# Attention and two FFNs on one core: keys scaled when they are copied, maxima that come out negated, and other numbers for the planner

## The chip, the cores and the metric

The kernel runs on one core of a Trainium2 chip. The time is device microseconds of one execution; lower is better. The times shown are the median of three runs, and one further execution was taken with the hardware profiler.

## What is computed

A block-sparse attention over 2 batches of 8 heads, 768 positions and 64 dimensions: each query sees the keys less than 16 positions away and one summary key for each block of 32 (the maximum over the block, with log 32 added to its score). Its output goes through two FFNs.

```python
scores_l = scale * np.matmul(q, k.transpose(0, 1, 3, 2))
scores_s = scale * np.einsum('bhsd,bhnd->bhsn', q, k_sum) + np.log(block)
scores_l_m = np.where(mask_l, scores_l, -1000000000.0)
scores_all = np.concatenate([scores_l_m, scores_s], axis=-1)
scores_all = scores_all - np.max(scores_all, axis=-1, keepdims=True)
a = np.exp(scores_all)
a = a / (np.sum(a, axis=-1, keepdims=True) + 1e-09)
out = np.matmul(a, np.concatenate([v, v_sum], axis=2))
...
h = x @ w_in1;  x = (h * np.cos(h)) @ w_out1
h = x @ w_in2;  x = (h * np.clip(h + 3.0, 0.0, 6.0) / 6.0) @ w_out2
```

The scale is 1/8. The FFNs run over 1536 rows, 512 wide, with 2048 hidden columns; every operand is split in a high and a low part (hi, lo), and a product is three matmuls.

## The kernel before

**Tiles.** The attention works on 12 tiles of 128 queries (`front(u)` and `back(u)`, u from 0 to 11), with all 8 heads in one tile. `front` loads the queries (`qt`), copies the windows of keys of the tile beside the block maxima into `kcat` (two buffers), and lets TensorE (PE) write mask plus scores into two PSUM banks: an identity product puts the mask there (L561), then 16 small matmuls add the scores (L574). DVE takes the maximum over each head's 120 columns (L595) and turns it into `nmx`, minus scale times the maximum (L596); ACT computes the exponentials with `nmx` as bias, one instruction for each head (L604); DVE computes the reciprocal sums (L610, L611), and POOL or DVE multiplies (L614). `back` transposes the result through PE (L629), copies it into `pts`, and multiplies with the values `vcat` (L644); the outcome is split in `xhi` and `xlo`. The maxima over blocks are taken once for each batch (`prep_k`, L477) and copied beside the keys (`put_k`, L483); the means of the values come from products with a small averaging matrix (`prep_v`, L519).

**FFN.** The steps `s` of the plan are (FFN, block of 512 rows, slice of 128 hidden columns). The first 12 steps are narrow: 256 rows each, on the first eight tiles of the attention, run while the attention goes on. Step s is `mm1` (L780, the hidden column slice), `middle` (on ACT a rounding L843, on DVE L845, on ACT the sine L847, on DVE a product L849, then the split into `ghe` and `gle`) and `mm2` (L898). From the 13th step on PE works 512 columns wide, and the second FFN uses seven products instead of eight for a pair of slices (L731). Weights are converted on the way (`raw` to `cv_y` and `cv_t` to the `phi`, `plo`, `whi_out`, `wlo_out` parts).

**ACT's tables.** The exponential and the sine are in different table sets, so ACT runs an `ACT_TABLE_LOAD` whenever it goes from one to the other.

**What sets the order.** Nearly all of the work is recorded as operations of a `Graph` (`G.op`): the engines that may run it with a cost for each, what it reads and writes, and sometimes a due time. `Graph.forward` plays the operations through a timetable of its own and picks, for each engine, which operation comes next; `run` then writes the instructions in the order of their planned starts. These numbers belong to it:

```python
    PATIENCE = {"ACT": 0.3, "POOL": 0.0}
    UNWANTED, SWITCH = 1.0, 8.0
...
                        if other <= t + cost:
                            continue
                        urge += self.UNWANTED
                    if e == "ACT" and self.ops[i][4] not in (None, table):
                        cost += self.TABLE
                        urge += self.SWITCH
```

An operation that DVE and another engine can both do goes to DVE only where the other would end later by more than its PATIENCE, and then it stands back by UNWANTED microseconds; an operation for ACT that needs the other table stands back by SWITCH. Loads are operations of the queue SP, which issues in the planned order. Where the timetable shows PE a gap of more than 0.3 us and a matmul, `fill` puts matmuls over a tile of zeros there (L868, L873); 12 more warm PE up (L468).

Of the kernel before, what the change touches and what calls it, by code (L numbers as in the profile page):

```python
# [22 lines left out]
P = 128  # L23
# [13 lines left out]
class Graph:  # L37
# [10 lines left out]
    SAME = 0.16  # L48
    DMA_LATENCY = 1.8
    FIRST_DMA = 1.7  # L50
    TABLE = 1.3


    PATIENCE = {"ACT": 0.3, "POOL": 0.0}
    UNWANTED, SWITCH = 1.0, 8.0

    def __init__(self):
        self.filler = None
# [30 lines left out]
    def forward(self, due, succ):  # L89
        n = len(self.ops)  # L90
        missing = [len(o[2]) for o in self.ops]
        begins, ends, on = [0.0] * n, [0.0] * n, [None] * n
        free, table, port = {"SP": self.FIRST_DMA}, "exp", 0.0
        ready = {i: self.at[i] for i in range(n) if not missing[i]}
        order = []

        def start(i, e, at):
            t = max(free.get(e, 0.0), at)
            return max(t, port) if e == "POOL" or (e == "DVE" and self.twice[i]) else t

        while ready:
            starts, first = [], {}
            for i, at in ready.items():
                engines = self.ops[i][0]
                other = 1e9
                if "DVE" in engines and len(engines) > 1:
                    other = min(start(i, e, at) + c - self.PATIENCE[e] for e, c in engines.items() if e != "DVE")
                for e, cost in engines.items():
                    t = start(i, e, at)
                    urge = due[i]  # L110
                    if e == "DVE" and other < 1e9:
# [6 lines that stand above are left out]
                    starts.append((urge, t, i, cost, e))  # L118
                    if t < first.get(e, 1e9):
                        first[e] = t  # L120
            e = min(first, key=lambda e: (first[e], e))
            limit = first[e] + (0.1 if e != "PE" else 0.05)
            _, t, i, cost, _ = min(x for x in starts if x[4] == e and x[1] <= limit)
            del ready[i]
            begins[i], ends[i], on[i] = t, t + cost, e
            free[e] = ends[i]
            if e == "POOL" or (e == "DVE" and self.twice[i]):
                port = max(port, ends[i])
            if e == "ACT" and self.ops[i][4]:
                table = self.ops[i][4]  # L130
            order.append(i)
            for j in succ[i]:
                missing[j] -= 1
                if not missing[j]:
                    ready[j] = max(ends[d] + self.delay(d, j, on) for d in self.ops[j][2])
        return begins, ends, on, sorted(order, key=lambda i: begins[i])
# [52 lines left out]
def attention_two_ffn(  # L189
# [124 lines left out]
    qt = ring(kv, "qt", NQ, [P, HP, P])  # L314
    es = ring(kv, "es", NE, [P, 2, HP, KC])
    pts = ring(kv, "pts", 2, [KC, H, P])
    small = {n: ring(kv, n, 2, [P, H]) for n in ("mx", "nmx", "sm", "sme", "rs")}


    zero = const.tile([P, P], F32R, name="zero")  # L320
    nc.vector.memset(zero.bitcast(F32), 0.0)
    mask = es[NE - 1].rearrange("p j h c -> p (j h) c")[:, 0:3, :]

    more = math.log(BLK) / scale
    few = math.floor(more * 64.0) / 64.0
    nc.gpsimd.memset(mask, few - more)
    nc.gpsimd.memset(mask[:, :, WK:KC], few)
# [137 lines left out]
    def wake(n):  # L465

        for _ in range(n):
            nc.tensor.matmul(bank["d0"], zero, zero.unsqueeze(1).to_broadcast([P, NK, P]), start=True, stop=True)  # L468

    def load_kt(b):  # L470
        for hp in range(HP):
            G.op({"SP": dma(P * S * 4)}, lambda e, hp=hp: nc.sync.dma_start(
                out=ktile[0][:, hp, :], in_=kt[b, :, hp, :]), w=[("kt", hp)])
# [6 lines left out]

    def put_k(b, i):
        n = HP * 2 * NB
        G.op({"DVE": dve(n, 2), "POOL": one(n)}, lambda e: VEC[e].tensor_copy(  # L483
            kcat[i][:, :, :, WK:KC], ksum[b].unsqueeze(2).to_broadcast([P, HP, 2, NB])
        ), r=[("ks", b, hp) for hp in range(HP)], w=[("kcs", i)], twice=True)

    def vstage(t):
# [58 lines left out]
    def front(u):  # L546
# [31 lines left out]
        for z0, z1 in groups:  # L578
# [2 lines left out]
                ap=[list(ktile[0].ap[0]), [S, z1 - z0], [a[1] - a[0], 2], [1, WK]],  # L581
            )
            n = (z1 - z0) * 2 * WK
            G.op({"ACT": act(n), "DVE": dve(n, 2), "POOL": one(n)}, lambda e, z0=z0, z1=z1, keys=keys: copy(
                e, kc[:, z0:z1, :, 0:WK], keys),
                r=[("kt", hp) for hp in range(z0, z1)], w=[("kcw", k, hp) for hp in range(z0, z1)], twice=True)
            G.op({"PE": 1.02 * (z1 - z0) / HP}, lambda e, z0=z0, z1=z1: scores(z0, z1),
                 r=[("qt", qi), ("kcs", k)] + [("kcw", k, hp) for hp in range(z0, z1)], w=spk)
        ef = es[ei].rearrange("p j h c -> p (j h) c")
        mx, nmx, sm, sme, rs = (small[n][si] for n in ("mx", "nmx", "sm", "sme", "rs"))  # L590
        ek = [("e", ei, 0), ("e", ei, 1)]

        def largest(e):
            for j in range(2):
                nc.vector.tensor_reduce(mx[:, j * HP:(j + 1) * HP], s4[j], AX.X, ALU.max)  # L595
            nc.vector.tensor_scalar(nmx, mx, -scale, None, ALU.mult)  # L596

        G.op({"DVE": dve(H * KC) + 0.27}, largest, r=spk, w=[("mx", si)])

        def power(e):  # L600
            for j in range(2):
                for hp in range(HP):
                    c = j * HP + hp
                    nc.scalar.activation(ef[:, c, :], s4[j][:, hp, :], AF.Exp, bias=nmx[:, c:c + 1], scale=scale,  # L604
                                         accum_out=sm[:, c:c + 1])

        G.op({"ACT": 2.75}, power, r=[("mx", si)] + spk, w=ek + [("sm", si)], table="exp")
# [516 lines left out]
```

## Time and profile before

| | |
|---|---|
| median of 3 runs | 601.85 us (601.09 to 602.21) |
| the profiled execution | 602.27 us |
| its span, first to last instruction | 600.5 us |
| PE busy in the span | 589.0 us (98%) |
| DVE, ACT, POOL busy | 466.7, 353.8, 169.4 us |
| granted TensorE clock | 1.00 throughout |

An engine's busy time is the part of the span in which one of its instructions runs; loads, waits and register instructions are not counted. A busy PE is not PE at its peak, since matmuls overlap; and the matmuls over zeros are busy time too. The span is 1.77 us shorter than the execution's own time.

### The profile page before, as it was taken

Reading aid. Unit: us, or ns where it says so; the run is one execution under the profiler, and the core shown is the slowest. Engines: PE = TensorE matmul, PEld = TensorE weight load, DVE = VectorE, ACT = ScalarE, POOL = GpSimd, SP = SyncE. Lnnn points to the kernel's source line nnn. Section 1 sums busy time; section 2 is a strip of 40 time slices with the busy share of each in tenths; the row PEclk is TensorE's granted clock in tenths of the full one; section 3 lists DMA queues with packets and bytes.
Section 4 is the critical chain, followed back from the end, with each engine's and each line's share of the span. In section 5 each row is a group of like instructions: output and inputs, shape, how many; then the busy total and the mean of one; then the engine's idle time right before and its main releaser. Section 6 shows DMA issues by size and latency. Waiting matters only on the chain.

```text
span 600.5 us, 10003 instructions
## 1 busy us (share of the span) xinstructions
PE 589.0 (98%) x3845; PEld 502.2 (84%) x3845; DVE 466.7 (78%) x823; ACT 353.8 (59%) x738; POOL 169.4 (28%) x170
## 2 busy tenths in 40 slices
PE   9989999999999999999999999999999999999997
PEld 6568799888888888888888898898988989899896
DVE  4899888998787687667576999989869984984544
ACT  3898999786555455445456567667655543552321
POOL 4166645241000110010054475251123311410110
PEclk9999999999999999999999999999999999999999
DMA  8586534334122123012100220233301310200111
GB/s 294 180 269 216 168 108 141 106 108 138 57 85 71 35 71 105 1 35 71 35 1 0 71 63 9 91 122 106 105 32 41 141 70 1 71 0 1 71 72 70
DMA packets 17008, 51.50 MB, mean 86 GB/s; under 512 B 1984, under 2 KB 1984, under 8 KB 16960
## 3 DMA queue, kind: packets, MB, share of 16 engines
q1 hardware_dynamic: 16960, 50.86, 25.3%
q8 instruction: 30, 0.49, 0.4%
q14 instruction: 18, 0.15, 0.1%
HBM read 47.71 MB, written 3.15 MB: 85 GB/s over the span
## 4 chain that ended last, share of the span: by engine, by line
PE 80%; DVE 9%; ACT 9%; issue 1%; POOL 0%; DVEq 0%; ACTq 0%; POOLq 0%
PE bank_a L898 20%; PE bank_d L780 10%; PE bank_b L898 9%; PE bank_c L898 9%; PE bank_d L731 9%; PE bank_c L780 5%; PE bank_e L780 5%; PE bank_e L731 5%; PE bank_c L731 4%; ACT es L604 3%; DVE ch_c L854 2%; DVE mx L595 1%; PE bank_e L519 1%; PE bank_d L468 1%; DVE total L936 1%; ACT L847 1%
## 5 line engine op out<-in xcount | busy, mean ns | idle before, releaser
L460 POOL TENSOR_TENSOR cv_y<-cv_t,cv_y 128x512 int32<-128x512 int32 x25 | 34.6, 1386 | 129.9 <-ACT cv_y L441 64.6
L400 POOL TENSOR_TENSOR plo<-cv_y,phi 128x512 fp32r<-128x512 f32 (+1 forms) x19 | 24.4, 1283 | 128.6 <-DVE phi L383 118.9
L852 ACT ACTIVATE ch_c<-hs,three 128x512 f32<-128x512 f32 x48 | 33.9, 720 | 28.2 <-DVE hs L744 27.3
L383 ACT CAST ghi<-ch_c 128x512 fp32r<-128x512 f32 x61 | 37.4, 619 | 18.7 <-DVE ch_c L849 10.5
L458 DVE SCALAR_TENSOR_TENSOR cv_t<-raw,cv_t 128x512 int32<-128x512 int32 x64 | 47.1, 746 | 0.5
L744 DVE TENSOR_TENSOR hs<-bank_d,hs 128x256 f32<-128x256 f32 x60 | 25.3, 421 | 22.9 <-PE bank_d L731 22.1
L441 ACT ACTIVATE cv_y<-raw 128x512 int32<-128x512 uint32 x55 | 36.9, 674 | 10.5 <-DVE wlo_out L400 4.1
L451 ACT ACTIVATE cv_t<-raw 128x512 f32<-128x512 f32 x56 | 37.6, 672 | 8.7 <-DVE plo L400 3.7
L858 DVE TENSOR_TENSOR glo<-ch_c,ghi 128x512 fp32r<-128x512 f32 x53 | 36.5, 695 | 7.1 <-ACT ghi L383 6.2
L854 DVE SCALAR_TENSOR_TENSOR ch_c<-ch_c,hs 128x512 f32<-128x512 f32 x48 | 39.2, 827 | 3.4 <-ACT ch_c L852 1.9
L780 PE MATMUL bank_d<-xhi,phi 128*128 128x512 f32 (+1 forms) x136 | 35.3, 358 | 1.2 <-DVE xhi L383 0.7
L456 DVE TENSOR_SCALAR cv_t<-cv_t 128x512 int32<-128x512 int32 x64 | 33.1, 521 | 3.4 <-ACT cv_t L451 3.2
L858 POOL TENSOR_TENSOR glo<-ch_c,ghi 128x512 fp32r<-128x512 f32 x12 | 16.3, 1367 | 59.6 <-ACT ghi L383 52.8
L780 PE MATMUL bank_d<-xlo,phi 128*128 128x512 f32 (+1 forms) x136 | 32.1, 354 | 0.0
L780 PE MATMUL bank_d<-xhi,plo 128*128 128x512 f32 (+1 forms) x136 | 31.7, 354 | 0.2 <-DVE plo L400 0.2
L460 DVE CUSTOM_DVE_ANT_0 cv_y<-cv_t,cv_y 128x1024 uint16<-128x1024 uint16 x39 | 28.0, 725 | 1.8 <-ACT cv_y L441 0.9
L604 ACT ACTIVATE es<-bank_c,nmx 128x120 f32<-128x120 f32 x80 | 27.6, 371 | 1.9 <-DVE nmx L596 1.5
L780 PEld LDWEIGHTS bank_d<-xhi,phi 128*128 128x128 f32 x136 | 22.9, 188 | 5.8 <-DVE xhi L383 0.9
L780 PEld LDWEIGHTS bank_d<-xhi,plo 128*128 128x128 f32 x136 | 23.1, 188 | 4.8 <-issue 0.8
L847 ACT ACTIVATE ch_c<-ch_c,half_pi 128x512 f32<-128x512 f32 x25 | 18.0, 722 | 14.7 <-DVE ch_c L845 14.7
L780 PEld LDWEIGHTS bank_d<-xlo,phi 128*128 128x128 f32 x136 | 23.2, 189 | 3.7 <-DVE xlo L660 0.2
L383 ACT COPY hs<-bank_d 128x256 f32<-128x256 f32 x24 | 8.9, 372 | 25.1 <-PE bank_d L731 24.9
(343 smaller groups left out, 1846.1 us busy)
## 6 DMA issues: line engine op xcount, KB each, us to landing
raw<-in_w_in_dram SPq DMA_DIRECT2D x32, 512.0 KB, 3.4
raw<-in_w_out_dram SPq DMA_DIRECT2D x32, 512.0 KB, 3.3
vcat<-in_vw_dram SPq DMA_DIRECT2D x12, 384.0 KB, 4.2
ktile<-in_kt_dram SPq DMA_DIRECT2D x8, 384.0 KB, 5.4
qt<-in_q_dram SPq DMA_DIRECT2D x12, 256.0 KB, 4.7
out_dram<-total SPq DMA_DIRECT2D x8, 256.0 KB, 2.0
total<-in_vw_dram SPq DMA_DIRECT2D x6, 256.0 KB, 4.5
out_dram<-totak SPq DMA_DIRECT2D x4, 256.0 KB, 2.0
```

Of the source, the lines that this page charges most:

```text
L383: nc.scalar.copy(o, i) if e == "ACT" else VEC[e].tensor_copy(o, i)
L441: nc.scalar.activation(y, low.bitcast(U32), AF.Copy, scale=2.0 ** -29)
L451: nc.scalar.activation(o, a, AF.Copy, scale=2.0 ** -112)
L458: G.op({"DVE": dve(DM)}, lambda e: nc.vector.scalar_tensor_tensor(t, high, -0x80000000, t, ALU.bitwise_and, ALU.bitwise_or), r=[rk], w=[tk ...
L460: G.op({"POOL": pool(DM), "DVE": dve(DM)}, lambda e: VEC[e].tensor_tensor(y, t, y, ALU.add), r=[tk], w=[yk], twice=True)
L604: nc.scalar.activation(ef[:, c, :], s4[j][:, hp, :], AF.Exp, bias=nmx[:, c:c + 1], scale=scale, accum_out=sm[:, c:c + 1])
L731: nc.tensor.matmul(o, wt[i][:, A[a], kk * P:(kk + 1) * P], xt[:, kk, :], start=first and n + kk == 0, stop=n + kk == 3, skip_group_check=True)
L780: nc.tensor.matmul(h, w["in"][i][:, kk * P:(kk + 1) * P], x[blk][:, kk, c0:c1], start=p + kk == 0, stop=p == 2 and kk == NK - 1)
L852: G.op({"ACT": act(N)}, lambda e: nc.scalar.activation(c(), h(), AF.Relu, bias=three), r=hk, w=ck)
L854: G.op({"DVE": dve(N)}, lambda e: nc.vector.scalar_tensor_tensor(c(), c(), 6.0, h(), ALU.min, ALU.mult), r=hk, w=ck, twice=bool(both))
L858: G.op({"DVE": dve(N), "POOL": pool(N)}, lambda e: VEC[e].tensor_tensor(gbuf("lo", s)[:, 0:N], c(), gh().bitcast(F32), ALU.subtract), r=[* ...
L898: nc.tensor.matmul(acc(s, i)[0], l, r, start=first, stop=end and p == 2 and (N == TOK or i % 2 == 1), skip_group_check=N < TOK)
```

## The change

The scale goes into the key copies: `scaled` multiplies by 1/8 where the keys and the block maxima are copied into `kcat` (an activation on ACT, a tensor_scalar on DVE or POOL). The scores then come out of PE scaled, the mask's constants are scaled with them, the exponential needs no scale, and the reduction writes the maxima negated at once into `nmx`; the instruction of L596 and the tile `mx` are gone. The planner's numbers change: an issue takes 0.45 us of SP's time and may run ahead of the wire by 3 us, PATIENCE is exchanged between ACT and POOL, UNWANTED goes from 1 to 10 and SWITCH from 8 to 2. Its cost for the maxima is 0.2 us lower.

```diff
@@ -48,11 +48,12 @@
+    ISSUE, RUN_AHEAD = 0.45, 3.0
     TABLE = 1.3
-    PATIENCE = {"ACT": 0.3, "POOL": 0.0}
-    UNWANTED, SWITCH = 1.0, 8.0
+    PATIENCE = {"ACT": 0.0, "POOL": 0.3}
+    UNWANTED, SWITCH = 10.0, 2.0
...
@@ -124,6 +125,10 @@
             free[e] = ends[i]
+            if e == "SP":
+
+                ends[i] = wire = max(wire, t) + cost
+                free[e] = max(t + self.ISSUE, wire - self.RUN_AHEAD)
             if e == "POOL" or (e == "DVE" and self.twice[i]):
...
-    more = math.log(BLK) / scale
+    more = math.log(BLK)
...
+    def scaled(e, o, i):
+
+        if e == "ACT":
+            nc.scalar.activation(o, i, AF.Copy, scale=scale)
+        else:
+            VEC[e].tensor_scalar(o, i, scale, None, ALU.mult)
...
-        G.op({"DVE": dve(n, 2), "POOL": one(n)}, lambda e: VEC[e].tensor_copy(
-            kcat[i][:, :, :, WK:KC], ksum[b].unsqueeze(2).to_broadcast([P, HP, 2, NB])
+        G.op({"DVE": dve(n, 2), "POOL": one(n)}, lambda e: scaled(
+            e, kcat[i][:, :, :, WK:KC], ksum[b].unsqueeze(2).to_broadcast([P, HP, 2, NB])
...
-            G.op({"ACT": act(n), "DVE": dve(n, 2), "POOL": one(n)}, lambda e, z0=z0, z1=z1, keys=keys: copy(
+            G.op({"ACT": act(n), "DVE": dve(n, 2), "POOL": one(n)}, lambda e, z0=z0, z1=z1, keys=keys: scaled(
...
-                nc.vector.tensor_reduce(mx[:, j * HP:(j + 1) * HP], s4[j], AX.X, ALU.max)
-            nc.vector.tensor_scalar(nmx, mx, -scale, None, ALU.mult)
-
-        G.op({"DVE": dve(H * KC) + 0.27}, largest, r=spk, w=[("mx", si)])
+                nc.vector.tensor_reduce(nmx[:, j * HP:(j + 1) * HP], s4[j], AX.X, ALU.max, negate=True)
+
+        G.op({"DVE": dve(H * KC) + 0.07}, largest, r=spk, w=[("mx", si)])
...
-                    nc.scalar.activation(ef[:, c, :], s4[j][:, hp, :], AF.Exp, bias=nmx[:, c:c + 1], scale=scale,
+                    nc.scalar.activation(ef[:, c, :], s4[j][:, hp, :], AF.Exp, bias=nmx[:, c:c + 1],
```

The planner's numbers move rows on every engine. Three places follow. The first is on PE, at the end of the first tile's scores; the products with `avg` are the means of the values. Before:

```order
L574 MATMUL bank_c_96<-kcat_124,qt_129 64x120
L574 MATMUL bank_c_97<-kcat_124,qt_129 64x120
L574 MATMUL bank_c_96<-kcat_124,qt_129 64x120
L574 MATMUL bank_c_97<-kcat_124,qt_129 64x120
L519 MATMUL bank_e<-vnat_122,avg 32x512
L519 MATMUL bank_e<-vnat_123,avg 32x512
L574 MATMUL bank_a_93<-kcat_125,qt_130 64x120
```

and of the change:

```order
L586 MATMUL bank_c_97<-kcat_124,qt_129 64x120
L531 MATMUL bank_e<-vnat_122,avg 32x512
L586 MATMUL bank_c_96<-kcat_124,qt_129 64x120
L586 MATMUL bank_c_97<-kcat_124,qt_129 64x120
L586 MATMUL bank_c_96<-kcat_124,qt_129 64x120
L586 MATMUL bank_c_97<-kcat_124,qt_129 64x120
L531 MATMUL bank_e<-vnat_123,avg 32x512
L586 MATMUL bank_a_93<-kcat_125,qt_130 64x120
```

One of the two mean products now stands ahead of the last four of the 16 score matmuls.

The second is on ACT, from the table load ahead of the ninth tile of the exponentials (counted from 0) to the end of the tenth; `ch_e` is a narrow step's hidden tile (rounding with `quarter`, sine with `half_pi`). Before:

```order
L604 ACT_TABLE_LOAD
L604 ACTIVATE es_132,sm_142<-bank_c_96,nmx_140 128x120 x4
L604 ACTIVATE es_132,sm_142<-bank_c_97,nmx_140 128x120 x4
L383 COPY pts_135<-bank_b 120x512
L383 COPY total_91<-bank_a_94 128x2x256
L843 ACTIVATE ch_e_103<-bank_d_98,quarter 128x256
L441 ACTIVATE cv_y_82<-raw_68 128x512
L441 ACTIVATE cv_y_81<-raw_67 128x512
L383 COPY pts_135<-bank_b 120x512
L383 CAST whi_out_76<-cv_y_82 128x512
L604 ACTIVATE es_133,sm_141<-bank_c_96,nmx_139 128x120 x4
L604 ACTIVATE es_133,sm_141<-bank_c_97,nmx_139 128x120 x4
```

and of the change:

```order
L615 ACT_TABLE_LOAD
L615 ACTIVATE es_132,sm_140<-bank_c_96,nmx_138 128x120 x4
L615 ACTIVATE es_132,sm_140<-bank_c_97,nmx_138 128x120 x4
L854 ACTIVATE ch_e_103<-bank_d_98,quarter 128x256
L388 COPY pts_135<-bank_b 120x512
L456 ACTIVATE cv_t_84<-raw_68 128x512
L858 ACT_TABLE_LOAD
L858 ACTIVATE ch_e_103<-ch_e_103,half_pi 128x256
L446 ACTIVATE cv_y_82<-raw_68 128x512
L615 ACT_TABLE_LOAD
L615 ACTIVATE es_133,sm_139<-bank_c_96,nmx_137 128x120 x4
L615 ACTIVATE es_133,sm_139<-bank_c_97,nmx_137 128x120 x4
```

A sine with a table load on either side now stands between the two tiles, and copies of `pts`, `total` and `whi_out` have left ACT. From the fifth tile on it is so for each tile; ACT has 16 table loads in place of 12.

The third is on PE, behind the scores of the last tile (`qt_131`). Before:

```order
L574 MATMUL bank_c_97<-kcat_125,qt_131 64x120
L629 MATMUL bank_b<-ident,es_132 120x128 x4
...
L644 MATMUL bank_e<-pts_136,vcat_128 64x64 x16
L780 MATMUL bank_d_98<-xhi_86,phi_69 128x256 x4
L780 MATMUL bank_d_98<-xhi_86,plo_71 128x256 x4
L780 MATMUL bank_d_98<-xlo_89,phi_69 128x256 x4
L780 MATMUL bank_d_99<-xhi_86,phi_69 128x256 x4
```

and of the change:

```order
L791 MATMUL bank_d_98<-xhi_86,plo_71 128x256 x4
L791 MATMUL bank_d_98<-xlo_89,phi_69 128x256 x4
L640 MATMUL bank_b<-ident,es_132 120x128 x4
...
L573 MATMUL bank_c_97<-mask_hi,ident_r 128x480
L586 MATMUL bank_c_96<-kcat_125,qt_131 64x120
...
L586 MATMUL bank_c_97<-kcat_125,qt_131 64x120
L655 MATMUL bank_e<-pts_136,vcat_128 64x64 x16
```

The narrow step in `bank_d_98` (the eleventh of twelve) and a group of four transposes have moved ahead of the last mask and scores.

## Rows read from the trace of the kernel before

**Rows 1.** Busy time by stretch: length, PE, weight loads, DVE, ACT, POOL, clock.
```profile
0.00:25.00 25.00, 22.75 (x165) 14.60 (x169) 13.32 (x25) 14.20 (x48) 6.91 (x34) 1.00 0.68 222
25.00:50.00 25.00, 22.31 (x314) 17.86 (x312) 23.70 (x46) 22.14 (x83) 14.68 (x14) 1.00 0.77 254
50.00:75.00 25.00, 24.22 (x314) 18.90 (x313) 22.83 (x45) 23.29 (x63) 15.82 (x19) 1.00 0.63 201
75.00:100.00 25.00, 24.72 (x330) 22.35 (x329) 21.86 (x49) 23.82 (x77) 11.11 (x10) 1.00 0.37 119
100.00:125.00 25.00, 24.70 (x199) 21.78 (x198) 21.97 (x42) 21.47 (x46) 11.15 (x9) 1.00 0.35 115
125.00:150.00 25.00, 25.00 (x112) 20.71 (x111) 22.70 (x38) 16.56 (x27) 5.49 (x4) 1.00 0.37 126
```

**Rows 2.** The chain that ended last, its start: start us, us, what.
```profile
7.78 3.43 PE bank_d L868 x15
...
12.19 1.83 PE bank_e L519 x4
```

**Rows 3.** PE's weight loads in order of time behind tile 10's exponentials.
```profile
93.64 0.19 PEld L561 LDWEIGHTS bank_c<-mask_hi,ident_r 128*128 128x128 f32 x1 [0.22 <-ACT es L604]
...
95.03 0.41 PEld L629 LDWEIGHTS bank_b<-ident,es 128*120 128x120 f32 x4 [0.16 <-issue]
```

**Rows 4.** ACT in order of time, at three places.
```profile
13.71 0.36 ACT L604 ACTIVATE es<-bank_c,nmx 128x120 f32<-128x120 f32 x1 [0.53 <-DVE nmx L596]
...
77.45 1.28 ACT L847 ACT_TABLE_LOAD   x1
78.75 0.51 ACT L847 ACTIVATE ch_e<-ch_e,half_pi 128x256 f32<-128x256 f32 x1
...
90.74 0.36 ACT L604 ACTIVATE es<-bank_c,nmx 128x120 f32<-128x120 f32 x1 [0.70 <-DVE nmx L596]
```

**Rows 5.** PE in order of time: a narrow step's twelve matmuls, and the first wide one.
```profile
98.24 0.74 PE L780 MATMUL bank_d<-xhi,phi 128*128 128x256 f32 x4
...
99.78 0.40 PE L780 MATMUL bank_d<-xhi,phi 128*128 128x256 f32 x2
...
111.76 1.09 PE L780 MATMUL bank_d<-xhi,phi 128*128 128x512 f32 x4
```

**Rows 6.** DVE's groups by form: count, busy us, mean ns, idle before.
```profile
L596 DVE TENSOR_SCALAR nmx<-mx 128x8 f32<-128x8 f32 x12 | 4.7, 389 | 0.4
L453 DVE TENSOR_SCALAR cv_t<-raw 128x512 f32<-128x512 f32 x8 | 4.4, 551 | 0.0
```

**Rows 7.** ACT's groups by form, the same columns.
```profile
L451 ACT ACTIVATE cv_t<-raw 128x512 f32<-128x512 f32 x56 | 37.6, 672 | 8.7 <-DVE plo L400 3.7 <-DMA raw<-in_w_in_dram 3.2 <-DMA raw<-in_w_out_dram 1.8
...
L847 ACT ACT_TABLE_LOAD x6 | 7.7, 1283 | 0.1
L383 ACT COPY pts<-bank_b 120x512 f32<-120x512 f32 x12 | 7.1, 594 | 0.0
...
L383 ACT COPY total<-bank_a 128x512 f32<-128x512 f32 x7 | 4.3, 615 | 0.2
...
L383 ACT COPY vcat<-vmean 24x1024 f32<-24x1024 f32 x2 | 2.1, 1044 | 0.0
...
L383 ACT COPY kcat<-ktile 128x768 f32<-128x768 f32 x2 | 1.7, 832 | 4.1 <-PE bank_c L574 4.1
```

**Rows 8.** DVE in order of time, tile 10's nmx.
```profile
89.36 1.29 DVE L596 TENSOR_SCALAR nmx<-mx 128x8 f32<-128x8 f32 x1
```

**Rows 9.** POOL in order of time, beside it.
```profile
88.09 2.52 POOL L460 TENSOR_TENSOR cv_y<-cv_t,cv_y 128x512 int32<-128x512 int32 x2 [6.60 <-ACT cv_y L441]
```

**Rows 10.** ACT's waits for nmx: us in total, times, longest.
```profile
ACT L604 <- DVE nmx L596: 1.5, 1, 1.5
ACT es L604 <- DVE nmx L596: 1.5, 3, 0.7
```

**Rows 11.** POOL's key copies, by form.
```profile
L383 POOL COPY kcat<-ktile 128x768 f32<-128x768 f32 x8 | 7.2, 903 | 9.7 <-PE bank_a L574 8.9 <-PE bank_c L574 0.7
```

More of the change, by code (lines that the diff above doesn't have):

```diff
@@ L92, in forward @@
         begins, ends, on = [0.0] * n, [0.0] * n, [None] * n
-        free, table, port = {"SP": self.FIRST_DMA}, "exp", 0.0
+        free, table, port, wire = {"SP": self.FIRST_DMA}, "exp", 0.0, 0.0
         ready = {i: self.at[i] for i in range(n) if not missing[i]}
@@ L316, in attention_two_ffn @@
     pts = ring(kv, "pts", 2, [KC, H, P])
-    small = {n: ring(kv, n, 2, [P, H]) for n in ("mx", "nmx", "sm", "sme", "rs")}
+    small = {n: ring(kv, n, 2, [P, H]) for n in ("nmx", "sm", "sme", "rs")}
     zero = const.tile([P, P], F32R, name="zero")
@@ L589, in front @@
         ef = es[ei].rearrange("p j h c -> p (j h) c")
-        mx, nmx, sm, sme, rs = (small[n][si] for n in ("mx", "nmx", "sm", "sme", "rs"))
+        nmx, sm, sme, rs = (small[n][si] for n in ("nmx", "sm", "sme", "rs"))
         ek = [("e", ei, 0), ("e", ei, 1)]
```

## The prediction

> **What bounds the kernel now.** I read the stretches first [rows 1]. From 125 us on TensorE (PE) is busy in 25.00 of 25 us at the full granted clock (1.00, 2.4 GHz), and the order of the work beside it can give nothing there. What is open lies in the first 125 us, the attention with the first FFN's narrow steps: PE is idle for 2.25, 2.69, 0.78, 0.28 and 0.30 us of the five stretches, 6.3 us in all. It also spends time on matmuls over a tile of zeros, which the planner puts wherever its own timetable shows PE a gap. Without the 12 of the warm-up these are 33 of 512 columns and 6 of 256. Fifteen of them take 3.43 us in the chain of waits [rows 2], 0.229 each, so the 33 are 7.6 us; half the columns put the others at 0.115 each (an estimate), 0.7 us. So 14.6 us of the attention are idle time or padding, and the rest is work that both kernels do.
>
> In the same stretches ACT is busy for 22.1, 23.3 and 23.8 of 25 us and DVE for 23.7, 22.8 and 21.9 [rows 1]: these two decide when PE gets its next operand. One link shows it. At 93.64 PE's weight load for the last mask product waits 0.22 us for ACT's exponentials of the tile before, because they read the score banks that the mask writes [rows 3]. Those exponentials began at 90.74 after 0.70 us of waiting for nmx [rows 4]. So ACT's queue up to there, plus what PE has left behind the last score, fixes when the wide FFN steps begin, at 111.76 [rows 5].
>
> **The change part by part.**
>
> *The table-driven order* is the large part, since the planner's numbers move every engine's rows, and I cost it along that link.
>
> (a) The start. PE's first scores now have a mean product between their third and fourth quarter (the order of PE's start shows it), and one more filler ahead. Two mean products take 1.83 us [rows 2], one 0.915, and a filler 0.23; the scores of tile 0 end at 12.19 + 1.15 = 13.34. Before, the first exponential followed their end by 13.71 - 12.19 = 1.52 us [rows 2, 4]. The removed nmx instruction with its hand-over was a fifth of a microsecond of that (an estimate; its mean of 0.389 [rows 6] holds waiting). First exponential at 14.65: **+0.95 us**. What hides nothing here: ACT then runs the exponentials of tiles 0 and 1 back to back, so the delay reaches them whole.
>
> (b) ACT's queue from there to the end of the exponentials of tile 10, counted in both orders. Four more table loads at 1.283 [rows 7]: +5.13. Five cv_t steps fewer at 0.672, two pts copies at 0.594, three total copies at 0.615, one vcat copy at 1.044: -7.44. One key copy more at 0.832, and single instructions of ghe, phi, sine and vmean more against one xhi and one whi_out less, by the same view's means: +1.76. Sum: **-0.55 us**. That the key copies become scaled activations I cost at nothing: an activation over 512 columns takes 0.672 [rows 7], a copy over 768 takes 0.832.
>
> (c) PE's rest behind the last score. Before, both narrow steps 10 and 11 (24 matmuls of L780) stood behind it; after, only step 11. Twelve such matmuls take 99.78 - 98.24 = 1.54 us, one group of four transposes fewer is 0.41 by its weight loads [rows 3, 5], and two 256-column fillers are gone, 0.23: **-2.2 us**.
>
> Sum of (a) to (c): 0.95 - 0.55 - 2.2 = -1.8 us, if ACT stands idle between 25 and 100 us as long as now, 5.75 us [rows 1]. Two things move that. It falls where the nmx instruction goes: ACT waited 3.0 us for it in four places, and DVE's nmx, 0.389 on average, took 1.29 us at 89.36 while POOL worked from 88.09 for 2.52 us [rows 6, 8, 9, 10]. It rises because DVE takes over six cv_t steps by the end of the attention (0.551 each, 3.3 us [rows 6]) and seven pts and total copies (about 0.6 each, by ACT's rows [rows 7]) against 4.7 us of nmx [rows 6] and two products handed to POOL, in stretches in which it is already 88 to 95% busy. The bounds of this term are -3.0 us (all nmx waits go, none comes) and +5.75 (ACT idle twice as long). I take **+0.3**, near the nearest rows: the waits saved are known, those added are not.
>
> *POOL.* It scales eight-head key tiles and the block maxima now; POOL's scaling of f32 has no row. Below: its plain copy, 0.903 for 768 elements [rows 11]. Above: its two-input sums, 2.52 for two of 512 columns [rows 9], 1.26 each and 1.9 us for 768. The maxima of the start land on POOL behind the last DVE maximum; the planner's filler covers PE until past 11.2 us [rows 2], so even the upper price costs nothing there; without that cover it would be up to 0.5 us. Later key tiles are made two tiles ahead and POOL is busy in 11 to 16 of 25 us [rows 1].
>
> *SP.* The planner lets issues run ahead; only their order changes, with the same transfers. All raw, q and v loads of the attention stay in front of their readers by several microseconds in both orders, except the first key loads, which stand first in both. Cost 0; the bound is a late q tile, some 0.5 us.
>
> *Negated reduction, unscaled exponent, constants.* The reductions keep shape and count; I take 0, as nothing else in them changes.
>
> *Padding.* Two fillers of 512 columns and six of 256 more, +1.15 us of PE time. They stand where the planner saw a gap, and (a) to (c) already count PE by what it waits for. If the gap weren't there, they'd cost that 1.15.
>
> *After 125 us* both orders hold the same matmuls and PE is full; 0, with ±0.5 for the second FFN.
>
> Total -1.8 + 0.3 = **-1.5 us**. The profiled execution took 602.27 (span 600.5 and 1.77 around it), 0.42 above the median of the runs; so 600.8 for such an execution, and 601.85 - 1.5 = 600.35, say **600.4 us** at the median.
>
> **A rule against it.** Behind a table load the trace shows nothing: it starts at 77.45, lasts 1.28, and the sine begins at 78.75 [rows 4]. The Trainium skill, "ScalarE: Activation LUTs", section "What ACT_TABLE_LOAD costs", puts a drain of about 1.38 us behind each load and 2.66 us on a switch, and under "Table sets" asks to do all the exps together; by its price the four added loads would cost 5.5 us more and the sum would be about +4.0. This case's rows disagree with the drain.
>
> **The rivals.**
>
> 1. *Larger gain.* The nmx waits go and no new ones come: -1.8 - 1.5 to -3.0, so -3.3 or more, 598.5 and below. For: in four places ACT stood for that one instruction [rows 10]. Against: DVE has little idle time to lend. Chance 0.12.
>
> 2. *No gain.* ACT's idle time rises by 1.5 us or the fillers push PE instead of filling it (+1.15): -0.6 to 0.6, 601.9. For: DVE at 95% in 25 to 50 us. Chance 0.27.
>
> 3. *Slower: the switches pace PE.* From tile 5 on every tile's exponentials stand between two loads of their own, behind a sine that needs a DVE step on the same bank. If the sine waits on DVE each time, the load and the exponentials behind it wait too, and PE with its mask product. Seven such pairs; from 0.45 us of waiting in each, about half the 0.70 at 90.74 [rows 4], the sum passes -1.8 + 3.2 = +1.4: 603.2. It decides from 0.26 us a pair, where the gain is zero. Against: the five pairs of before stand in 75 us in which ACT is idle for only 5.75 in all [rows 1]. Chance 0.14.
>
> 4. *Slower: a switch holds ACT for longer than its load*, by as much again: four times 1.28 is 5.1, sum +3.6, 605.5. Load and sine stand 0.02 us apart [rows 4]. Chance 0.02. This is the rule named above.
>
> **How the numbers follow.** The forecast, a gain of 0.6 to 3.3 us, has 0.45. A measurement of this kernel can tell about 0.2%, 1.2 us, from no change. Of the forecast case 0.30 lies beyond 1.2 us, with rival 1 that makes faster 0.42; its other 0.15 and 0.22 of rival 2 make the same, 0.37; rivals 3 and 4 and the edge of 2 make slower, 0.21. The forecast's own range is 598.6 to 601.3; the range over the cases goes from 598.4 (rival 1's upper half) to 603.0 (most of rival 3).
>
> **What would show it.** Right: first exponential near 14.6 us; ACT with 16 table loads, no row of nmx's own; tile 10's exponentials ending within half a microsecond of 93.6; the first 512-column L780 (now L791) near 110.2; PE idle plus filler of the first 125 us at about 13 us. Step (b) is wrong if the end of those exponentials moves by more than a microsecond, (c) if PE stands waiting behind the last score. The prediction fails if waits of ACT's sines for DVE, or of PE for gle and wlo (POOL and DVE), add up to more than 2 us, or if PE loses time in the second FFN, where both orders differ too.

## The result, and the profile after

The changed kernel takes 607.35 us (median of 6, 605.20 to 608.00) against 601.15 us for the kernel before on the same chip: a ratio of 1.009, 95% interval 1.007 to 1.011. It is 6 us slower; 600.4 was forecast, and the range ended at 603.0. Of the six executions four have a mean granted clock of 0.997 and take 607.27 to 608.00, the other two (0.998 and 0.999) take 605.20 and 605.35. The profiled execution took 607.42 us at 0.997, its span is 605.6.

The same view as [rows 1], busy time by stretch (length, PE, weight loads, DVE, ACT, POOL, clock), of the changed kernel:

```profile
0.00:25.00 25.00, 23.66 (x198) 15.11 (x200) 13.49 (x24) 13.58 (x47) 12.25 (x37) 1.00 0.83 265
25.00:50.00 25.00, 21.04 (x279) 16.91 (x280) 24.36 (x41) 21.25 (x79) 18.62 (x12) 1.00 0.73 239
50.00:75.00 25.00, 23.16 (x255) 19.05 (x254) 21.88 (x45) 18.67 (x54) 13.27 (x14) 0.93 0.52 162
75.00:100.00 25.00, 23.66 (x326) 21.50 (x325) 21.13 (x41) 24.65 (x71) 18.30 (x17) 1.00 0.41 122
100.00:125.00 25.00, 25.00 (x257) 22.28 (x257) 23.31 (x45) 22.76 (x50) 11.67 (x12) 1.00 0.34 111
...
350.00:375.00 25.00, 23.57 (x149) 20.87 (x149) 23.73 (x37) 16.71 (x32) 10.95 (x8) 1.00 0.13 43
375.00:400.00 25.00, 24.51 (x154) 21.75 (x153) 22.27 (x41) 16.34 (x31) 10.08 (x9) 1.00 0.27 85
```

PE's idle time in the first 125 us rose from 6.3 to 8.5 us, and POOL, for which PE waited 0.3 us in all there before, is busy for 44.1 us in the first 75 in place of 37.4. In one stretch the granted clock is below 1.00. And there is idle time far behind 125 us, in the second FFN.

To add things up I cut each trace at two rows of PE: the first score product and the first 512-wide product of the first FFN. They are here for the changed kernel, with the scores of the last tile between them:

```profile
10.77 0.84 PE L586 MATMUL bank_c<-kcat,qt 64*64 64x120 f32 x24
...
100.31 1.05 PE L586 MATMUL bank_c<-kcat,qt 64*64 64x120 f32 x32
...
114.88 1.14 PE L791 MATMUL bank_d<-xhi,phi 128*128 128x512 f32 x4
```

and two such rows of the kernel before; its first wide product is in [rows 5]:

```profile
11.14 1.05 PE L574 MATMUL bank_c<-kcat,qt 64*64 64x120 f32 x32
...
94.05 1.05 PE L574 MATMUL bank_c<-kcat,qt 64*64 64x120 f32 x32
```

The attention took 100.62 us before (11.14 to 111.76) and takes 104.11; the rest, from the first wide product to the end of the span, took 488.70 and takes 490.77. So 3.5 us were lost in the attention, 2.1 behind it, and 0.4 were won at the start: 5.2, which is what the two spans (600.46 and 605.65) differ by.

The cut is also what makes the experiments readable. Four kernels below (e4, e8, f1, f2) have the same code and the same order in the attention and differ behind it; they show 98.69, 98.72, 98.73 and 98.71 us for it, while whole executions of one kernel differ by one to two microseconds.

### The profile page after: what moved, and what is told of

It reads as the page before. It is cut to its first block, busy times and chain, and to the rows that moved or that the text cites. A ratio compares the mean times of both kernels' runs of the same rounds, so it can differ in the third digit from the quotient of the medians.

```text
span 605.6 us, 9999 instructions
## 1 busy us (share of the span) xinstructions
PE 590.0 (97%) x3853; PEld 504.3 (83%) x3853; DVE 468.5 (77%) x812; ACT 351.2 (58%) x727; POOL 190.3 (31%) x184
## 4 chain that ended last, share of the span: by engine, by line
PE 81%; DVE 11%; ACT 5%; POOL 1%; issue 1%; DVEq 0%; POOLq 0%; ACTq 0%
PE bank_a L909 21%; PE bank_d L791 11%; PE bank_b L909 9%; PE bank_c L909 9%; PE bank_d L742 9%; PE bank_e L791 4%; PE bank_c L791 4%; PE bank_e L742 4%; PE bank_c L742 4%; DVE ch_c L865 2%; ACT es L615 1%; PE bank_e L655 1%; DVE cv_t L463 1%; PE bank_d L473 1%; DVE total L947 1%; PE bank_c L586 1%
## 5 line engine op out<-in xcount | busy, mean ns | idle before, releaser
L465 POOL TENSOR_TENSOR cv_y<-cv_t,cv_y 128x512 int32<-128x512 int32 x26 | 36.8, 1416 | 116.6 <-ACT cv_y L446 56.1
L463 DVE SCALAR_TENSOR_TENSOR cv_t<-raw,cv_t 128x512 int32<-128x512 int32 x64 | 49.2, 778 | 0.5
L865 DVE SCALAR_TENSOR_TENSOR ch_c<-ch_c,hs 128x512 f32<-128x512 f32 x48 | 36.3, 772 | 5.1 <-ACT ch_c L863 3.3
L456 ACT ACTIVATE cv_t<-raw 128x512 f32<-128x512 f32 x46 | 30.9, 671 | 6.0 <-DMA raw<-in_w_in_dram 2.5
L461 DVE TENSOR_SCALAR cv_t<-cv_t 128x512 int32<-128x512 int32 x64 | 31.8, 499 | 1.6 <-ACT cv_t L456 1.4
L947 DVE SCALAR_TENSOR_TENSOR total<-bank_a,total 128x512 f32<-128x512 f32 x22 | 14.8, 687 | 10.6 <-PE bank_a L909 10.6
```

The source lines that it names most:

```text
L461: G.op({"DVE": dve(DM, 2)}, lambda e: nc.vector.tensor_scalar(t, t, 3, None, ALU.logical_shift_left), w=[tk], twice=True)
L463: G.op({"DVE": dve(DM)}, lambda e: nc.vector.scalar_tensor_tensor(t, high, -0x80000000, t, ALU.bitwise_and, ALU.bitwise_or), r=[rk], w=[tk ...
L465: G.op({"POOL": pool(DM), "DVE": dve(DM)}, lambda e: VEC[e].tensor_tensor(y, t, y, ALU.add), r=[tk], w=[yk], twice=True)
L865: G.op({"DVE": dve(N)}, lambda e: nc.vector.scalar_tensor_tensor(c(), c(), 6.0, h(), ALU.min, ALU.mult), r=hk, w=ck, twice=bool(both))
```

## The experiments

Two theories stood at the start. **A**: the loss is POOL's scaling, 2.18 us for an eight-head key tile where the copy took 0.90 [rows 11], and what queues behind it. **B**: the loss is the new order. POOL's groups by form in the changed kernel, its first 125 us (count, busy us, mean ns, idle before):

```profile
L480 POOL TENSOR_SCALAR kcat<-ktile 128x768 f32<-128x768 f32 x6 | 13.1, 2177 | 11.3 <-PE bank_a L586 6.0 <-PE bank_c L586 5.2
L480 POOL TENSOR_SCALAR kcat<-ktile 128x192 f32<-128x192 f32 x4 | 2.7, 690 | 0.3 <-DMA ktile<-in_kt_dram 0.2
```

All results; attention and rest are the two stretches defined above, in the profiled execution. The ratio is against the kernel before on the same chip, whose medians there were 601.11 to 601.61 us; the 601.85 of the first row is the median from ahead of the prediction.

| kernel | what it is | attention | rest | median | ratio to before |
|---|---|---|---|---|---|
| before | | 100.62 | 488.70 | 601.85 | |
| changed | | 104.11 | 490.77 | 607.35 | 1.009 (1.007 to 1.011) |
| e1 | new code, old numbers | 105.26 | 488.81 | 606.85 | 1.0097 (1.0079 to 1.0115) |
| e2 | old code, new numbers | 104.62 | 490.76 | 607.68 | 1.0097 (1.0078 to 1.0115) |
| f3 | old code in the changed order | 103.09 | 490.74 | 606.51 | 1.0093 (1.0077 to 1.0110) |
| e3 | changed, POOL copies plainly | 100.45 | 490.76 | 603.39 | 1.0033 (1.0022 to 1.0045) |
| e5 | changed, padding in one gap | 102.64 | 490.77 | 605.81 | 1.0079 (1.0064 to 1.0094) |
| e4 | changed, POOL's scaling priced | 98.69 | 490.77 | 601.45 | 1.0002 (0.9993 to 1.0010) |
| e6 | e4 with the nmx instruction | 100.68 | 490.68 | 603.23 | 1.0036 (1.0024 to 1.0049) |
| e8 | e4, second FFN ordered as before | 98.72 | 488.70 | 599.43 | 0.9970 (0.9958 to 0.9982) |
| e12 | e8, POOL copies plainly | 98.66 | 488.71 | 599.58 | 0.9968 (0.9957 to 0.9979) |
| f1 | e8, only PATIENCE old there | 98.73 | 490.89 | 601.78 | 1.0012 (1.0003 to 1.0021) |
| f2 | e8, only UNWANTED old there | 98.71 | 490.33 | 601.66 | 1.0013 (0.9997 to 1.0028) |
| e7 | e4 with UNWANTED 1 throughout | 103.63 | 491.89 | 607.27 | 1.0101 (1.0086 to 1.0116) |
| e9 | e8 with SWITCH 8 | 100.46 | 488.83 | 601.46 | 0.9999 (0.9989 to 1.0009) |
| e10 | e8 without the run-ahead | 103.04 | 488.71 | 603.18 | 1.0025 (1.0014 to 1.0035) |
| e11 | e1 with POOL's scaling priced | 98.14 | 488.82 | 599.17 | 0.9959 (0.9943 to 0.9975) |

### Each half alone: e1 and e2

e1 takes the changed code and puts the planner's numbers back:

```diff
-    PATIENCE = {"ACT": 0.0, "POOL": 0.3}
-    UNWANTED, SWITCH = 10.0, 2.0
+    PATIENCE = {"ACT": 0.3, "POOL": 0.0}
+    UNWANTED, SWITCH = 1.0, 8.0
...
-                ends[i] = wire = max(wire, t) + cost
-                free[e] = max(t + self.ISSUE, wire - self.RUN_AHEAD)
```

> The scaled key copies and the negated maxima with the planner's numbers of before (and its cost for the maxima of the change). Theory A (the loss is POOL's scaling, 2.18 us for an eight-head key tile against 0.90 for the copy, and what queues behind it on POOL): most of the 6 us of loss is here too, 605 to 607. Theory B (the loss is the new order, which the planner's numbers make): 601 to 602.5, POOL's scaling hidden or paid by the nmx instruction that is gone.

e2 takes the code of before with the new numbers (the same lines the other way round).

> The planner's new numbers with the key copies, the nmx instruction and the constants of before. Theory A: 601 to 602.5, since POOL copies without scaling. Theory B: 604 to 607, with PE waiting for DVE near 50 us and in the second FFN (about 2 us more idle after 300 us than before).

Each half alone loses as much as both together, so neither theory holds by itself: e1 spoke for A, e2 for B. What e1's loss is made of, its time doesn't tell: POOL scales four eight-head tiles there in place of six, and PE's largest wait in its attention is for DVE's es, 3.5 us in three places. The rest is clear from these two already: it is 488.8 with the old numbers and 490.8 with the new ones, whatever the code.

### The price of POOL's scaling at a fixed order: e3

```diff
         if e == "ACT":
             nc.scalar.activation(o, i, AF.Copy, scale=scale)
+        elif e == "POOL":
+            nc.gpsimd.tensor_copy(o, i)
         else:
```

> The changed kernel, its order unchanged row by row, but where POOL scales keys or block maxima it copies without the scale (the scaling is left out there, so scores of those tiles are eight times as large). Theory A: PE's idle time of the first 125 us falls from 8.5 to about 6 us, the fall of the clock near 54 us goes too, 602 to 603. Theory B: at most the 0.84 us wait for plo at 28 us goes; 605.5 to 606.5.

The attention is 3.66 us shorter, the time 4.0. One mechanism shows at 27 us. POOL and PE in order of time, in the changed kernel:

```profile
25.09 2.13 POOL L480 TENSOR_SCALAR kcat<-ktile 128x768 f32<-128x768 f32 x1
27.18 1.27 POOL L405 TENSOR_TENSOR plo<-cv_y,phi 128x512 fp32r<-128x512 f32 x1
...
28.51 0.74 PE L791 MATMUL bank_d<-xhi,plo 128*128 128x256 f32 x4 [0.84 <-POOL plo L405]
```

and POOL and PE in e3, row for row the same queues:

```profile
24.32 0.82 POOL L480 COPY kcat<-ktile 128x768 f32<-128x768 f32 x1
25.10 1.28 POOL L405 TENSOR_TENSOR plo<-cv_y,phi 128x512 fp32r<-128x512 f32 x1
...
26.75 0.64 PE L793 MATMUL bank_d<-xhi,plo 128*128 128x256 f32 x4
```

The key tile itself is early enough. Behind it in POOL's queue stands a low weight part that PE needs at once; it comes 1.3 us later than with the copy in front, and PE's wait of 0.84 us for it is gone. That is not all of the 3.66 us. Counted from the first score product, PE is 1.0 us behind e3 after this wait, 1.9 at 53 us, 3.4 at 61 us (the next section has the cause of this part) and 3.7 at the first wide product. The 0.9 us between 28 and 53 us go for the most part with DVE: three of its short steps last 0.6 us longer than in e3, each beside a scaling on POOL: at 28.76 and 46.97 us 1.05 for 0.42, at 30.06 us 0.79 for 0.17. The first of them, and POOL beside it, in the changed kernel:

```profile
28.76 1.05 DVE L448 TENSOR_SCALAR cv_y<-raw 128x512 int32<-128x512 uint32 x1
```
```profile
28.42 2.40 POOL L480 TENSOR_SCALAR kcat<-ktile 128x768 f32<-128x768 f32 x1
```

Behind the step at 46.97 stand the rest of cv_t, POOL's cv_y and ACT's phi, for which PE waits at 51.02. No run separates this way from the queue's. Theory A is right on this order, but e3 still isn't as fast as the kernel before.

### The clock: e5

PE in order of time, and its clock (third number of the lower rows) in the changed kernel:

```profile
51.02 0.74 PE L791 MATMUL bank_d<-xhi,phi 128*128 128x256 f32 x4 [0.36 <-ACT phi L388]
53.25 0.82 PE L791 MATMUL bank_d<-xhi,phi 128*128 128x256 f32 x4 [1.48 <-DVE ch_e L860]
53.86 1.06 PE L791 MATMUL bank_d<-xhi,plo 128*128 128x256 f32 x4
```
```profile
53.80:57.10 3.30, 3.30 (x18) 0.50 0.64 197
57.20:60.00 2.80, 2.80 (x72) 1.00 0.64 260
```

Behind two waits close together (0.36 and 1.48 us) PE was granted 0.50, that is 1.2 GHz, for at least 3.3 us; four products of 256 columns take 1.06 us there. e5 fills the second gap:

```diff
             self.ops[i][1](on[i])
+            if i == 363:
+                self.filler(6)
```

> The changed kernel with 1.4 us of matmuls over zeros more on PE, in the place where PE stood idle for 1.48 us at 51.8 us and after which the clock was granted at 0.50 for 3.4 us; nothing else moves. If the half clock is a part of POOL's price: the clock stays at 1.00, the first 512-wide product comes at about 113.2 in place of 114.88, the time falls by 1.7 us to about 605.5. If the stretch at half clock is hidden by other waits: the first wide product within 0.3 us of 114.88, 607.

PE in e5 at that place, and the clock behind it:

```profile
51.62 1.59 PE L886 MATMUL bank_a<-zero 128*128 128x256 f32 x12
53.27 0.74 PE L793 MATMUL bank_d<-xhi,phi 128*128 128x256 f32 x4
53.84 0.64 PE L793 MATMUL bank_d<-xhi,plo 128*128 128x256 f32 x4
```
```profile
54.00:58.00 4.00, 4.00 (x77) 1.00 0.67 222
```

The product behind the gap starts at the same time, 53.27 for 53.25, but at full clock, and the four behind it take 0.64 us. The attention is 1.47 us shorter and the time 1.5: of the 3.66 us that e3 gives back, 1.47 are the clock's and 2.19 are left for the scaling at full clock. What decides whether it falls stays open: in e3 PE is idle for 1.39 us ahead of the same product and keeps its clock (PE in e3, and the clock behind it):

```profile
50.57 0.74 PE L793 MATMUL bank_d<-xhi,phi 128*128 128x256 f32 x4 [1.39 <-DVE ch_e L862]
```
```profile
50.50:54.50 4.00, 3.93 (x56) 1.00 0.74 217
```

e2's profiled execution has such a fall as well (0.56 and 0.59 from 44 to 48 us), so its 104.62 holds the clock's price too.

### The planner told the price: e4

```diff
+def mul(n):
+    return 0.19 + 2.58e-3 * n
...
-            G.op({"ACT": act(n), "DVE": dve(n, 2), "POOL": one(n)}, lambda e, z0=z0, z1=z1, keys=keys: scaled(
+            G.op({"ACT": act(n), "DVE": dve(n, 2), "POOL": mul(n)}, lambda e, z0=z0, z1=z1, keys=keys: scaled(
```

(and the same for the block maxima).

> The changed kernel with the planner told what POOL's scaling takes here: 2.17 us for an eight-head tile and 0.69 for a quarter, in place of 1.11 and 0.36; the order follows. Theory A: the planner moves work off POOL, 601 to 603. Theory B: no better than the changed kernel, 605 to 608, since the other numbers still order DVE and ACT.

The attention falls to 98.69, 2 us under before; the 2.07 us lost behind it keep the time level.

### What the removed instruction is worth: e6 and f3

e6 puts the small negation back behind each reduction, in e4's order:

```diff
-                nc.vector.tensor_reduce(nmx[:, j * HP:(j + 1) * HP], s4[j], AX.X, ALU.max, negate=True)
+                nc.vector.tensor_reduce(mx[:, j * HP:(j + 1) * HP], s4[j], AX.X, ALU.max)
+            nc.vector.tensor_scalar(nmx, mx, -1.0, None, ALU.mult)
```

> The kernel with POOL's scaling priced (e4), the same order, with the small negation of the maxima put back behind each reduction (times minus one). What it costs is what the removed instruction is worth at a fixed order: if it stands on ACT's path in each tile, 12 times 0.2 to 0.4, first wide product 2 to 3.5 us later than e4's 109.78, time 603.5 to 605; if DVE and ACT have slack there, under 0.7 us, 601.5 to 602.

It costs 1.99 us of the attention and 1.8 of the time, at the lower edge of the first case. f3 is e2 with the change's cost of the maxima (0.07 for 0.27), which gives the changed order row by row:

> The code of before (copies without scale, the nmx instruction, the exponential's scale) in the changed kernel's order, row by row: e2 with the change's cost of the maxima. Against e3 (the same order without nmx, POOL copying without scale, 603.4) it shows what the nmx instruction costs there; against before, what the order alone does. If nmx is worth 1.8 us as it was in e4's order: 605.2. If e2's 607.7 was due to nmx in this kind of order: 607 or more.

606.51 us was measured, between the two cases named. f3 closes the sum for the attention. The changed order alone takes the old code from 100.62 to 103.09 (+2.47), the removed instruction and the copies' new kind on ACT and DVE from there to 100.45 (e3, -2.64), and POOL's scaling to 104.11 (+3.66, the fall of the clock included).

### The second FFN: e8, f1, f2, e7

From 290 us of the planner's time on, e8 takes PATIENCE and UNWANTED of before; its second FFN has the order of before row by row, its attention that of e4.

```diff
+    PATIENCE_LATE, UNWANTED_LATE = {"ACT": 0.3, "POOL": 0.0}, 1.0
...
-                        urge += self.UNWANTED
+                        urge += self.UNWANTED_LATE if at > 290.0 else self.UNWANTED
```

> The kernel with POOL's scaling priced (e4), and from 290 us of the planner's time on PATIENCE and UNWANTED of before: the attention's order is e4's, the second FFN's row by row that of before. If the two parts add: first wide product at 109.8, 488.7 us from there to the end of the span, time 599.4, 2 us faster than both kernels. If the second FFN's waits come from where the attention leaves off and not from its order: 490.8 for that stretch, 601.4.

599.43 was measured: the parts add, and this is 0.3% under the kernel before. What PE waits for behind 300 us (us in total, times, longest), first in the changed kernel, then in e8:

```profile
PE bank_e L742 <- DVE hs L755: 1.4, 2, 0.9
PE bank_d L742 <- DVE txlo L709: 0.6, 1, 0.6
PE bank_d L742 <- DVE hs L755: 0.6, 1, 0.6
PE bank_c L742 <- DVE hs L755: 0.5, 1, 0.5
```
```profile
PE bank_a L916 <- DVE wlo_out L412: 0.5, 1, 0.5
PE bank_e L749 <- DVE hs L762: 0.2, 1, 0.2
PE bank_d L749 <- DVE hs L762: 0.2, 1, 0.2
```

The longest of these in the changed kernel, DVE in order of time ahead of it, and PE:

```profile
351.33 1.78 DVE L959 TENSOR_TENSOR xlo<-total,xhi 128x512 fp32r<-128x512 f32 x1
353.03 1.78 DVE L463 SCALAR_TENSOR_TENSOR cv_t<-raw,cv_t 128x512 int32<-128x512 int32 x1
354.74 0.41 DVE L755 TENSOR_TENSOR hs<-bank_e,hs 128x256 f32<-128x256 f32 x1
```
```profile
355.20 0.51 PE L742 MATMUL bank_e<-xhi,phi 128*128 128x256 f32 x2 [0.85 <-DVE hs L755]
```

The sum that frees PE's bank stands behind two steps that PE isn't waiting for, each 1.78 us long. Such a step takes 0.68 us elsewhere in this trace (the next cv_t at 357.71); beside each of the two POOL was at work, from 351.08 for 1.47 us and from 352.52 for 1.74.

f1 and f2 take one of the two numbers back each, in the second FFN alone.

> The kernel of e8 with only PATIENCE of before in the second FFN, UNWANTED there at 10 as in the change. If ACT's PATIENCE made the 2.05 us: from the first wide product to the end of the span 488.7 to 489.2, 599.4. If UNWANTED made them: 490.5 or more, 601.4.

> The kernel of e8 with only UNWANTED of before in the second FFN, PATIENCE there as in the change. e7 had this pair everywhere and took 491.9 us for that stretch, 3.4 us of it at half clock. If PATIENCE is the cause: 490.5 or more again, 601.5 to 602.5. If UNWANTED: 488.7 to 489.2, 599.4.

f1 speaks for UNWANTED and f2 for PATIENCE: each taken back alone leaves the stretch at 490.89 and 490.33. So the loss can't be put down to one number by these runs; the pair of before gives a good order here and each mixture tried a worse one. The waits differ too: f1 keeps those for hs, f2 has one long one:

```profile
360.86 0.74 PE L916 MATMUL bank_a<-wlo_out,ghi 128*128 128x512 f32 x2 [1.83 <-DVE wlo_out L412]
```

e7 sets UNWANTED to 1 throughout, over e4.

> The kernel with POOL's scaling priced (e4) and UNWANTED back at 1. If UNWANTED alone makes the 2.05 us that the second FFN loses in every kernel with the new numbers (488.7 us from the first wide product to the end of the span before, 490.75 to 490.8 after): that stretch takes 488.7 to 489.2, the attention may go either way by a microsecond; 599 to 601. If ACT's PATIENCE makes it: the stretch stays at 490.5 or more.

Its attention, expected to move by a microsecond, took 4.9 us longer than e4's, with one planner number moved and the right price. Its second FFN is f2's and has the same wait; there the clock fell behind it, and the stretch is 1.56 us longer than f2's (PE's busy time and clock):

```profile
364.00:366.00 2.00, 0.83 (x5) 1.00 0.00 0
366.00:368.00 2.00, 2.00 (x13) 0.55 0.00 0
368.00:370.00 2.00, 2.00 (x7) 0.60 0.00 0
```

### Does the price still matter, and do the new numbers: e12, e9, e10, e11

e12 is e8 with e3's edit.

> The kernel of e8, its order unchanged row by row, but where POOL scales it copies without the scale (left out there, so the scores of those tiles are eight times as large). What POOL's scaling still costs once the planner knows of it: if nothing waits for POOL any more, within 0.4 us of e8, 599.0 to 599.8; if as much as in the changed kernel, 4 us less, 595.5.

0.06 us of the attention: once the order allows for it, POOL's scaling costs nothing. The planner leaves POOL three of the eight-head tiles in e8, in place of six. e9 and e10 undo one of the other numbers in e8.

> The kernel of e8 (POOL's scaling priced, second FFN in the order of before; 599.4) with SWITCH back at 8; 16 table loads as there, other rows moved. If it matters little which of two orders the planner finds once its prices are right: within 1 us of e8, 598.5 to 600.5. If switching early is what e8 lives on: 601 or more.

> The kernel of e8 without the run-ahead of SP (an issue holds the queue until its transfer is through, as before). If the loads of the attention are early enough either way, as the prediction had it: within 0.6 us of e8, 598.8 to 600. If the run-ahead carries a part of e8's gain: 600.5 or more, with waits for DMA in the first 40 us.

Both lost more than I thought: 1.7 and 4.3 us of the attention, the latter with one fall of the clock. The waits for DMA that I expected in e10 aren't there: between its first score and its first wide product no engine waits for one, and PE's longest wait is 1.43 us for DVE's es at 103 us. So the loads came in time, and the order is what got worse. Still the numbers are not needed for such a gain, since e11 has none of them:

> All the planner's numbers of before, the scaled copies and the negated maxima, and POOL's scaling priced (e1 with the price). If the missing price alone made e1 slow: first wide product from 115.2 back to 108 to 111, 597.5 to 600.5. If the old numbers can't order the new code well either: 603 or more.

e11 is the fastest of all, 599.17, with 14 table loads; and it hands POOL more of the slow scalings than the changed kernel does, seven against six:

```profile
L484 POOL TENSOR_SCALAR kcat<-ktile 128x768 f32<-128x768 f32 x7 | 15.6, 2223 | 7.2 <-PE bank_a L590 5.5 <-PE bank_c L590 1.6
```

In e4's order the gain is the code's: 1.93 us under before, and e6 gives 1.99 of them back. In e11's order the code's share wasn't measured. For the same code and right prices the planner's orders gave 98.14, 98.69, 100.46, 103.04 and 103.63 us, and the choice of these numbers moves the time as much as the whole change does.

## Why the prediction was wrong, step by step

**POOL's scaling at nothing** is the step that failed, worth +3.66 us at the changed order (e3), of which 1.47 came by a fall of the clock (e5). Two things were wrong in it. The upper bound was 1.9 us, from sums of two inputs; the scaling takes 2.18, more than either row that I bounded it by. And the cover was read off the wrong thing: that key tiles are made two tiles ahead and that POOL is busy 11 to 16 of 25 us says when the tile is needed and how full POOL is, not what stands behind the tile in POOL's queue. That was plo at 28 us, with PE waiting for it, 1.0 of the 3.66 us. The bound should have been carried on to what is queued behind.

**The planner's price** I had in front of me and didn't use: the change leaves POOL's scaling at the copy's cost (`one(n)`, 1.11 us for 768 columns), so the order was made for an instruction that no longer exists.

**After 125 us, 0 ± 0.5** failed as well: +2.07. That PE is full from 125 to 325 us holds in both traces; the second FFN was given half a microsecond on no row at all, though the numbers changed its order of DVE and ACT as they changed the attention's. The last sentence of the prediction named it as a way to fail.

**(a) to (c) and ACT's idle time.** Without POOL's scaling, e3 against before, the attention changed by -0.17 us where -1.5 was forecast. The forecast's large part, the order, has the wrong sign: it costs the old code 2.47 us (f3), and the removed instruction with the copies' new kind gives 2.64 back. (c) was right and too small: from the last tile's scores to the first wide product before took 17.71 us, after 14.57, so -3.1 for -2.2. (a) was nearly right: the first exponential starts 2.57 us behind the first score before (13.71 [rows 4] less 11.14) and 3.10 behind it after (13.87 less 10.77), so +0.5, where the forecast's +0.95 less the filler ahead of the scores (0.23) makes +0.7. The term that I took at +0.3, ACT's idle time from 25 to 100 us, went from 5.75 to 6.9 us in e3 and to 10.43 in the changed kernel, near its upper bound; the exponentials of tile 10 end at 99.7 in place of 93.6; their last one in the changed kernel:

```profile
99.35 0.39 ACT L615 ACTIVATE es<-bank_c,nmx 128x120 f32<-128x120 f32 x1
```

How ACT and PE came to wait shows ahead of PE's longest wait, DVE in order of time, and POOL beside the first row:

```profile
49.20 1.15 DVE L621 TENSOR_SCALAR sme<-sm 128x8 f32<-128x8 f32 x1
...
50.50 1.76 DVE L489 TENSOR_REDUCE ksum<-ktile 128x24 f32<-128x768 f32 x2
52.18 0.68 DVE L388 CAST xhi<-bank_e 128x512 fp32r<-128x512 f32 x1
52.78 0.41 DVE L860 TENSOR_TENSOR ch_e<-bank_d,ch_e 128x256 f32<-128x256 f32 x1
```
```profile
49.03 1.29 POOL L465 TENSOR_TENSOR cv_y<-cv_t,cv_y 128x512 int32<-128x512 int32 x1 [1.29 <-DVE cv_t L463]
```

The product ch_e that PE and ACT wait for stands behind an instruction on eight columns that takes 1.15 us while POOL works, and behind two maxima of the next batch. On average sme takes 523 ns, before 279; in e3 it takes 443, so most of the rise is the order's. The Trainium skill, "SBUF — State Buffer", section "Who interferes with whom", has VectorE in its two-port modes and GpSimd share one pair of ports by an exclusive lock, the second to come waiting for the whole instruction. The trace agrees: the POOL sum beside it began first, at 49.03, and sme, which takes 0.16 us where it is free, ends within 0.03 us of it.

**The removed nmx** was in my sum only as waits of ACT, 3.0 us at most. Measured at e4's order it is worth 1.99 us (e6), inside that bound; it is the part of the change that wins.

**The rivals.** The switches didn't pace PE: 16 table loads stand in e4 and e8 too, at 98.7 us. Nor does a switch hold ACT longer than its load, in the changed kernel as before:

```profile
85.12 1.28 ACT L858 ACT_TABLE_LOAD   x1
86.41 0.51 ACT L858 ACTIVATE ch_e<-ch_e,half_pi 128x256 f32<-128x256 f32 x1
```

The drain behind the load that the Trainium skill, "ScalarE: Activation LUTs", "What ACT_TABLE_LOAD costs", prices at 1.38 us shows in none of these rows. Of the changed kernel's 16 loads 15 have ACT's next instruction 0.01 us behind them; behind the first, at the start, it comes 2.2 us later. The slow case that happened, a costlier instruction on an engine with time to spare, was not among the rivals.

**What stays open:** why the same planner makes a 98 us order from one set of numbers and a 104 us one from another. e1 against e11 differs in the one price and gains 7.1 us, but the scatter of the orders alone is 5.5, so that figure is not the price's worth; at fixed orders that worth is 3.66 us (e3) and 0.06 (e12). What makes the clock fall behind gaps of 1.4 to 1.8 us in some traces and executions and not in others is open too.

## What to carry to other kernels

When an edit changes the kind of an instruction, measure it on each engine that may run it and put it into the planner's prices in the same change: here the new code in the planner's old numbers lost 5.3 us with the old price (e1) and won 2.4 with the right one (e11), though the scatter of orders is a part of that. What a slower instruction costs is looked for in what is queued behind it on its engine and in the steps of other engines beside it, not in how busy that engine is. A new set of planner numbers is judged at a fixed code, and a new code at a fixed order; otherwise the scatter of orders, some 5 us here, passes for the effect.

## What was unexpected of the hardware

POOL takes 2.18 us to scale 768 f32 columns and 0.82 to 0.90 to copy them; the scaling costs 2.6 ns for each further column (2177 less 690 ns over 576 columns). For the same tile ACT takes 0.86 scaled and 0.83 plain, and DVE 0.55 scaled (e3) and 0.54 plain (f3), so only POOL's price changed much.

The start isn't the same in each execution. All these kernels begin with the same 12 products over zeros. PE in order of time behind them, in the kernel before, the changed one and e11:

```profile
6.34 1.00 PE L561 MATMUL bank_c<-mask_hi,ident_r 128*128 128x480 f32 x2
```
```profile
6.17 0.59 PE L573 MATMUL bank_c<-mask_hi,ident_r 128*128 128x480 f32 x2
```
```profile
5.23 0.60 PE L577 MATMUL bank_c<-mask_hi,ident_r 128*128 128x480 f32 x2
```

The two mask products take 1.00 us in one trace and 0.59 in another. A 512-wide product over zeros starts every 0.43 us at first and every 0.23 later; the rate changes at 3.8 us of the span in e11, at 5.9 in the changed kernel and at 7.1 before, while the rows give the granted clock as 1.00 all along. So the 12 products take 4.4 to 5.5 us, and the first score starts anywhere from 9.6 to 11.1. This is a microsecond or more between executions, and the reason for counting from the first score.
